# One-hot groups split around the scores, their multiply on GpSimd, and low weight halves kept in DRAM for the second dense stage

## The chip, the cores and the metric

The kernel runs on one core of a Trainium2 chip. A core has five engines that each work through their own instruction queue in order: TensorE (PE; its weight loads are shown apart as PEld), VectorE (DVE), ScalarE (ACT), GpSimd (POOL) and SyncE (SP), which here only issues DMAs. They meet through semaphores alone. The metric is the device time of one execution in microseconds (us).

## The reference

A layer norm feeds two branches, and their outputs and the input are added.

- Attention: S = 2048 positions, D = 512, 32 query heads of width 16 that share one key and one value head; exact softmax over all 2048 keys, then the product with `wo`.
- A product-key mixture of 4096 small experts (PEER): per position and head two scores over 64 keys each, the best two of each, the best two of their four sums; a softmax over these two gives the gates `g`. Each position so has 64 (expert, gate) pairs, and `out = sum g * gelu(x . u[e]) * v[e]`.

```python
act = _gelu(jnp.einsum("nd,nhkd->nhk", xf, ue))      # ue = u[top_e]
out = jnp.einsum("nhk,nhk,nhkd->nd", g, act, ve)     # ve = v[top_e]
return x + _A_ref(xn, ...) + _B_ref(xn, ...)
```

## The kernel before, in words

**Two ways through the experts.** The 2048 positions are four groups of 512. For groups 0 and 1 the experts are gathered: for each of 512 slots an indirect DMA from POOL's queue (L976, `gather`) brings 128 rows of u and v, DVE takes the dot product (L988, `dot`), ACT the tanh, and DVE adds the weighted v to the sum (L1023, `add`). Twelve buffers hold gathered rows; a gather waits until an add has freed one. For groups 2 and 3 the experts are computed densely (`dense`, run once with `DG` = 2 and once with `DG` = 3): all 4096 experts in `NB` = 32 blocks of 128, each block being 12 matmuls for the activations (L733), the gelu times a gate matrix, and the matmuls with v (L861).

**Halves.** Float32 products are made of faster fp32r matmuls: a tensor is split into a high half (a rounded copy) and a low half (what is left), and three of the four products are summed. For the expert weights `half_split` (L694) does this: ACT copies the high half out of the raw tile `rw` (L697), DVE subtracts to get the low one (L698). There are 64 such splits in each dense stage (u and v of 32 blocks). `fetch` (L664, L665) loads the raw tiles, two blocks ahead; with two buffers it has to wait until both engines are through with the tile that it overwrites.

**The gate matrix** of a dense stage is made at its start, in the one-hot stage. 512 positions are taken in `NQ` = 32 groups of `TB` = 16. For each group `onehot(q)` builds on DVE two one-hot tensors in fp16: `oa`, 128 x 2048 (L783), and `ob`, 128 x 512 (L785), and multiplies `ob` by the gate (L786). Then 16 small matmuls of 32 columns each (L815, `pg`) form the gate columns, and ACT copies the result out (L820). `onehot(q + 2)` is written two groups ahead of its matmuls; `obs` has three places for `ob`. When the gates are complete they go to DRAM, and the blocks follow.

**Order.** From the start of the attention loop on, the order on every engine is written out by hand. The loop has 256 steps of two key chunks. `att_steps` writes for each step: four scores matmuls (L326) and their two exponentials on ACT (L329), the 16 probability-times-value matmuls (L340, `pv`), then `mid()` (dots, tanh, deferred work), four scores matmuls and two exponentials again, then `fill()`. `fill` takes pieces of the expert work off the generator `score_thread` until its planned cost has caught up with a planned line (`aim`) or 4.0 (`MOST`) has been spent in this step. A one-hot group costs 2.0, so that a step of the one-hot stage (`dense_on[0] == 2`) takes two groups, both behind the second four scores matmuls. In that stage the adds and the next gathers (`go`) stand behind `fill`. Scores have two PSUM buffers, so a scores matmul waits for the exponential two before it.

Of the kernel before, what the change touches and what calls it, by code (L numbers as in the profile page):

```python
# [11 lines left out]
F32 = mybir.dt.float32  # L12
# [6 lines left out]
OP = mybir.AluOpType  # L19
# [4 lines left out]
P = 128  # L24
# [12 lines left out]
NSP = 2  # L37
NB = 32
# [12 lines left out]
MOST = 4.0  # L51
# [4 lines left out]
def tile_kernel(ctx, tc, x, wq, wkv, wo, wqT, kT, uv, ub, vb, out):  # L56
    nc = tc.nc
    pool = lambda name, **kw: ctx.enter_context(tc.tile_pool(name=name, **kw))
    dram = pool("dram", bufs=1, space=DRAM)
# [9 lines left out]
    raw = lambda ap: ap.bitcast(F32)  # L69
# [10 lines left out]
    d_m = dram.tile([2, H, S], F32, name="dm")  # L80
    d_sum = dram.tile([15, 8, 512], F32, name="dsum")
    d_inv = dram.tile([15, 8, 512], F32, name="dinv")
    d_part = [dram.tile([P, D], F32, name=f"dpart{t}") for t in range(NT)]


# [285 lines left out]
    def pair_load(pp):  # L371
        rc = small.tile([P, 32], F32, name="rc", bufs=1)
        nc.sync.dma_start(rc, d_sum[pp].rearrange("h n -> (h n)").rearrange("(p n) -> p n", n=32))
        RC[pp] = rc
# [68 lines left out]
    def out_ready():  # L443
        return PWO and GT * QB[PWO[0][0]] + PWO[0][1] in LIVE
# [28 lines left out]
    def wk_tile():  # L473
        return big.tile([P, 2, 512], F32R, name="wk", tag="wk", bufs=NWK)
# [181 lines left out]
    def dense(DG, after):  # L656
# [38 lines left out]
        def half_split(b, i):  # L695
            rw, w = raws[b], wk_tile()
            nc.scalar.copy(w[:, 0, :], rw[:, i, :])  # L697
            behind(lambda: nc.vector.tensor_tensor(out=w[:, 1, :], in0=rw[:, i, :], in1=w[:, 0, :], op=OP.subtract))  # L698
            return w

        def split(b):
# [74 lines left out]
        bc = lambda n, tb, w: tr[:, n, None, tb:tb + TB].to_broadcast([P, w, TB])  # L776
        OH = {}

        def onehot(q):
            if q < NQ:  # L780
                tb = q * TB
                oa = kt(F16, (P, P, TB))
                nc.vector.tensor_tensor(out=oa, in0=io, in1=bc(0, tb, P), op=OP.is_equal)  # L783
                ob = obs[:, q % 3]
                nc.vector.tensor_tensor(out=ob, in0=io[:, :NB, :], in1=bc(1, tb, NB), op=OP.is_equal)  # L785
                nc.vector.tensor_mul(ob, ob, bc(2, tb, NB))  # L786
                OH[q] = oa, ob

        def first_gates():
# [17 lines left out]
        for q in range(NQ):  # L807
# [4 lines left out]
            oa, ob = OH.pop(q)  # L812
# [223 lines left out]
    def dots(to):  # L1036
        while d_next[0] < min(to, NSL):
            dot(d_next[0])
            d_next[0] += 1
# [16 lines left out]
    store = STORES.append  # L1056
    on_act, behind = ON_ACT.append, BEHIND.append

    def run(fns):
        todo = fns[:]  # L1060
        fns.clear()
        for fn in todo:
            fn()

    def posts():
        while POST:
            for fn in POST.pop(0):
                fn()
# [50 lines left out]
    dense_on, quiet = [0], [0]  # L1119
    sgen = score_thread()  # L1120
    spent = [0.0]

    def run_scores(until=None, key=None):
        while (until is not None and spent[0] < until) or (key is not None and key not in IDX):
            posts()
            try:
                cost = next(sgen)
            except StopIteration:
                spent[0] = 1e9
                posts()  # L1130
                return
            if cost is None:

                if key is None:
                    return
                continue
            spent[0] += cost

    STEPS = 512


    def att_steps(d, mid, fill):
        i = 2 * d
        run(STORES)
        if 144 <= i < STEPS and i % 128 == 16:
            PWO.extend((i // 128 - 1, j) for j in range(4))
        if i < STEPS:
            u, kc = divmod(i, 16)
            if i == 0:
                load_q(0, rows=False)  # L1150
                run_scores(until=spent[0] + 1.8)
            if kc == 4 and u + 1 < 32:
                load_q(u + 1)
            scores(u, kc, 0)
            scores(u, kc, 1)
        if 0 < i <= STEPS:
            pu, pk = divmod(i - 2, 16)
            pv(pu, pk)
            pv(pu, pk + 1)
            if pk == 14:  # L1160
                unit_tail(pu)
        mid()
        if i < STEPS:
            scores(u, kc + 1, 0)
            scores(u, kc + 1, 1)
        if out_ready() and (i % 128 >= HOLD and PWO[0][0] != 1 or i % 128 >= 32 and i % 4 == 0 and PWO[0][0] == 1):
            block_out()
            spent[0] += 3.6
        fill()

        pp, r = divmod(i, 32)
        if pp and pp < 16:
            if r == 4:
                pair_load(pp - 1)
            if r == 6:
                pair_invert(pp - 1)
            if r == 10:
                pair_spread(pp - 1)
# [12 lines left out]
        if i == STEPS - 6:  # L1191
            load_last()
# [55 lines left out]
    with tc.manual_schedule(engines={E_.PE, E_.Activation, E_.DVE, E_.Pool, E_.SP}):  # L1248
        done0 = spent[0]
        half = STEPS // 2  # L1250
        pos, since = 0.0, half
        for d in range(half + 24):


            if dense_on[0] != 0:
                since = d
            if dense_on[0] == 1:
                pos += 2.6 if d < half * 3 // 4 else max(0.0, NSL - pos) / max(half - 3 - d, 1)
            else:
                pos += (2.1 if len(IDX) < NC * TPH else 2.3 if 0 <= d - since < 12 else 1.75, 0, 1.4, 1.5, 0.5)[dense_on[0]]  # L1260

            todo = max(min(int(pos + 0.001), g_next[0]) - d_next[0], 0)

            def mid():
                post = POST[:]
                POST.clear()
                for act, _ in post:
                    act()
                tanhs(d_next[0])
                run(ON_ACT)  # L1270
                ON_ACT.extend(LATER_ACT)
                LATER_ACT.clear()
                run(LAST)
                LAST.extend(LATER)
                LATER.clear()
                rest = BEHIND[:]
                BEHIND.clear()

                dots(d_next[0] + todo - 1)
                if a_ready[0] > a_next[0]:  # L1280
                    weigh(a_next[0] // SB)
                dots(d_next[0] + 1 if todo > 0 else 0)
                for _, fn in post:
                    fn()
                sums = min(a_ready[0] - a_next[0], max(todo, 3) if d < half else 4)
                if dense_on[0] > 2:
                    sums = min(sums, 2)
                if quiet[0] > 0:
                    quiet[0] -= 1
                    sums = 0  # L1290
                if dense_on[0] == 2:
                    run(CHAIN)

                def go():
                    n = sums
                    while rest or CHAIN or n > 0:
                        if n > 0:
                            adds(1)
                            n -= 1
                        elif not rest:  # L1300
                            run(CHAIN)
                        if CHAIN:
                            CHAIN.pop(0)()
                        if rest:
                            rest.pop(0)()
                    gathers(4)

                    for _ in range(1 if d < half - 4 else NT):
                        if OUTS:
                            experts_out(OUTS.pop(0))  # L1310

                if dense_on[0] == 2:
                    POST_FILL.append(go)
                else:
                    go()

            aim = done0 + (FILL - done0) * (d + 1) / half if d < half else 1e6

            def fill():
                run_scores(until=min(aim, spent[0] + MOST))  # L1320
                run(POST_FILL)

            att_steps(d, mid, fill)
        flush()
        run(STORES)
        while a_next[0] < NSL:
            dots(NSL)
            run(CHAIN)
            tanhs(d_next[0])
            adds(SB)  # L1330
            run(STORES)
            gathers(NGB)
        assert not OUTS
        run(STORES)
# [37 lines left out]
```

## Time and profile before

| | |
|---|---|
| median of 3 runs | 1931.54 us (1929.22 to 1931.95) |
| the profiled execution | 1925.78 us, span of its instructions 1924.1 us |
| PE, DVE, ACT, POOL busy | 97%, 85%, 67%, 36% of the span |
| first dense stage: one-hot groups | about 608 to 707 us |
| first dense stage: blocks | about 707 to 1100 us |
| second dense stage: one-hot groups | about 1413 to 1523 us |
| second dense stage: blocks | about 1523 to 1860 us |

The span runs from the first instruction to the last. Busy time of an engine is the time that it spends in instructions, waiting for operands within one included; a busy PE is not a PE at its peak. PEclk is the share of the TensorE clock that was granted. A line of groups reads: line, engine, operation, output<-input, shapes, count | busy us, mean ns of one | idle time before them and what ended it. A window line reads: window, its length, and for each engine busy us and (number of instructions).

### The profile page before, as it was taken

To read this page: it belongs to the slowest core of one execution; us is meant where nothing else is said; L and a number is where in the kernel's file an instruction comes from. 1 tells how busy PE (TensorE), PEld (TensorE's weight loads), DVE (VectorE), ACT (ScalarE), POOL (GpSimd) and SP (SyncE) were. 2 spreads that over 40 slices of the span, in tenths; PEclk is the share of its full clock that TensorE was granted. 3 is DMA by queue.
4 is the path that set the end of the run, shared out by engine and by line. 5 is a ranking of instruction groups with operands and counts; after the bars stand their busy time and mean duration, and the time that the engine had idled before them with its cause. 6 is when DMAs were issued, how large, how long until landed. Compare 5 with 4: busy or idle time off the path is not lost.

```text
span 1924.1 us, 34929 instructions
## 1 busy us (share of the span) xinstructions
PE 1863.8 (97%) x10990; PEld 991.8 (52%) x10990; DVE 1634.0 (85%) x6381; ACT 1294.2 (67%) x1803; POOL 700.8 (36%) x920
## 2 busy tenths in 40 slices
PE   6979999999999999999999999999999999999998
PEld 3634444555555554555555554555555455555553
DVE  6627787989998977999999897899988779999994
ACT  3346666655557887787877555555578777888873
POOL 1203334434452223343444444355422134344430
PEclk9989999999999899999999999999988899999999
DMA  7857789787773778888999987876736778899882
GB/s 274 315 186 278 266 272 301 279 296 251 249 246 122 233 240 249 253 288 270 287 300 309 362 287 237 280 256 220 242 105 220 249 215 292 271 284 286 282 277 84
DMA packets 234395, 491.13 MB, mean 255 GB/s; under 512 B 93396, under 2 KB 93396, under 8 KB 234204
## 3 DMA queue, kind: packets, MB, share of 16 engines
q0 software_dynamic: 73728, 268.47, 42.0%
q1 hardware_dynamic: 159240, 219.56, 34.9%
q8 instruction: 88, 1.44, 0.3%
q10 hardware_dynamic: 1236, 0.82, 0.1%
q14 instruction: 103, 0.84, 0.1%
HBM read 427.41 MB, written 56.07 MB: 251 GB/s over the span
## 4 chain that ended last, share of the span: by engine, by line
PE 85%; DMA 3%; ACT 3%; DVE 1%; issue 1%; SPq 0%; DVEq 0%; ACTq 0%
PE pv L340 24%; PE psc L531 18%; PE sc L326 17%; PE pact L733 9%; PE pout L861 9%; PE pg L815 3%; PE pwo L433 2%; ACT pt L329 2%; PE pw L486 1%; DMA wqt<-in_wqT_dram 1%; DMA dinv<-rc 1%; DMA wk<-dw 1%; PE pwt L493 0%; PE pwl L408 0%; DMA qa<-dqh 0%
## 5 line engine op out<-in xcount | busy, mean ns | idle before, releaser
L329 ACT ACTIVATE pt<-sc 128x1024 f32<-128x1024 f32 x1024 | 993.7, 1026 | 461.9 <-PE sc L326 460.5
L976 POOL DMA_INDIRECT g<-in_uv_dram,idx x512 | 556.8, 1087 | 1002.0 <-DVE xa L1023 531.0
L340 PE MATMUL pv<-pt,vaug 128*32 128x512 f32 x4096 | 516.4, 623 | 0.0
L531 PE MATMUL psc<-wk,xt 128*128 128x512 f32 x1536 | 388.7, 401 | 4.1 <-DVE wk L496 3.5
L326 PE MATMUL sc<-qa,kaug 64*128 64x512 f32 x2048 | 384.2, 451 | 8.6 <-ACT pt L329 8.4
L1023 DVE SCALAR_TENSOR_TENSOR xa<-g,w,xa 128x512 f32<-128x512 f32 x512 | 371.7, 744 | 0.1
L988 DVE CUSTOM_DVE_ANT_0 g<-g,xa 128x512 f32<-128x512 f32 x512 | 335.5, 681 | 7.4 <-DMA g<-in_uv_dram,idx 7.4
L531 PEld LDWEIGHTS psc<-wk,xt 128*128 128x128 f32 x1536 | 277.9, 188 | 107.7 <-issue 37.5
L326 PEld LDWEIGHTS sc<-qa,kaug 64*128 64x128 f32 x2048 | 155.9, 185 | 329.3 <-ACT pt L329 218.8
L340 PEld LDWEIGHTS pv<-pt,vaug 128*32 128x32 f32 x4096 | 109.6, 111 | 257.0 <-issue 255.4
L546 DVE FIND_INDEX8 i<-m,psc 128x8 uint32<-128x64 f32 x1024 | 206.3, 220 | 0.0
L733 PE MATMUL pact<-xt,wk 128*128 128x512 f32 x768 | 195.9, 400 | 0.0
L861 PE MATMUL pout<-wk,wd 128*128 128x512 f32 x768 | 194.8, 401 | 0.2 <-DVE wd L919 0.2
L544 DVE MAX8 m<-psc 128x8 f32<-128x64 f32 x1024 | 146.2, 213 | 41.1 <-PE psc L531 40.3
L861 PEld LDWEIGHTS pout<-wk,wd 128*128 128x128 f32 x768 | 140.8, 188 | 47.3 <-DVE act L988 5.5
L733 PEld LDWEIGHTS pact<-xt,wk 128*128 128x128 f32 x768 | 139.4, 188 | 48.5 <-issue 17.5
L698 DVE TENSOR_TENSOR wk<-rw,wk 128x512 fp32r<-128x512 f32 x128 | 84.8, 683 | 9.7 <-ACT wk L697 9.7
L864 DVE TENSOR_TENSOR da<-da,pout 128x512 f32<-128x512 f32 x128 | 82.8, 679 | 10.1 <-PE pout L861 10.0
L783 DVE TENSOR_TENSOR oh<-oh 128x2048 f16<-128x2048 f16 x64 | 78.0, 1219 | 0.8 <-ACT oh L759 0.6
L815 PEld LDWEIGHTS <-oh 128*128 128x128 f16 x1024 | 68.4, 162 | 13.8 <-issue 6.4
L1011 DVE SCALAR_TENSOR_TENSOR w<-gth,ga 128x4 f32<-128x4 f32 x128 | 20.4, 159 | 64.5 <-ACT gth L1004 64.0
L815 PE MATMUL pg<-oh 128*128 128x32 f16 x1024 | 73.5, 247 | 0.6 <-DVE oh L786 0.5
(159 smaller groups left out, 1411.1 us busy)
## 6 DMA issues: line engine op xcount, KB each, us to landing
wk<-dw SPq DMA_DIRECT2D x96, 512.0 KB
wqt<-in_wqT_dram SPq DMA_DIRECT2D x32, 512.0 KB
dw<-wk SPq DMA_DIRECT2D x32, 512.0 KB
rw<-in_ub_dram SPq DMA_DIRECT2D x64, 256.0 KB
rw<-in_vb_dram SPq DMA_DIRECT2D x64, 256.0 KB
gy<-dg SPq DMA_DIRECT2D x64, 256.0 KB
qa<-dqh SPq DMA_DIRECT2D x128, 64.0 KB
g<-in_uv_dram,idx POOLq DMA_INDIRECT x512, 6.0
```

What stands on the lines that cost most here:

```text
L326: nc.tensor.matmul(p[:, b, :], kaug[o:o + 64, kc * P:(kc + 1) * P], QA[u][o:o + 64, i, :], start=True, stop=True)
L329: nc.scalar.activation(pt, p, AF.Exp, scale=SCALE)
L340: nc.tensor.matmul(PV[u][32 * j:32 * j + 32, :], vaug[:, kc, :], pt[:, b, :], start=kc == 0, stop=kc == 15)
L531: nc.tensor.matmul(p, XT[g][k][:, a, j * P:(j + 1) * P], WC[n_][k][:, bb, :], start=n == 0, stop=n == 11)
L544: nc.vector.max(m8[:, jb, s, :], p[:, s * E:(s + 1) * E])
L546: nc.vector.max_index(i8[:, jb, s, :], m8[:, jb, s, :], p[:, s * E:(s + 1) * E])
L733: nc.tensor.matmul(p, us[:, a, k * P:(k + 1) * P], XT[DG][k][:, c, :], start=n == 0, stop=n == 11)
L815: nc.tensor.matmul(p[:, i * NB:(i + 1) * NB], oa[:, :, i], ob[:, :, i], start=True, stop=True)
L861: nc.tensor.matmul(p, wd[0][:, a, j * P:(j + 1) * P], vs[:, c, :], start=n == 0, stop=n == 5)
L976: nc.gpsimd.indirect_dma_start(out=gt, out_offset=None, in_=uv, in_offset=bass.IndirectOffsetOnAxis(ap=IDX[ph, c, ti][:, s:s + 1], axis=0))
L988: nc.vector.tensor_tensor_reduce(u, u, XN[TPH * ph + ti], scale=1.0, scalar=0.0, op0=OP.mult, op1=OP.add, accum_out=a[:, i:i + 1])
L1023: nc.vector.scalar_tensor_tensor(acc, v, w[:, i:i + 1], acc, op0=OP.mult, op1=OP.add)
```

## The change

Three things are changed, and no arithmetic.

1. In `onehot` the multiplication of `ob` by the gate is issued on GpSimd instead of VectorE: 64 instructions of 128 x 512 fp16, in place. It waits for the comparison that writes `ob`, and the group's small matmuls wait for it. In POOL's queue the 64 stand among the gathers.
2. In the one-hot stage a step's first group moves ahead of the second four scores matmuls: a new callback `between()` takes one piece off the generator there, and `fill` takes what is left of 4.0. PE's order in a step becomes scores, pv, group, scores, group; ACT's order stays as it was.
3. With `DG` = 2 each low half is also stored to a new DRAM tensor `d_lo` (64 DMAs of 256 KB, queued through `store` for the start of the next step). With `DG` = 3 the low half is loaded from there (64 DMAs of 256 KB from SP's queue) and the 64 subtractions on VectorE go. The raw weights are still loaded, for ACT's copy of the high half.

```diff
+    d_lo = dram.tile([NB, P, 2, 512], F32, name="dlo")
...
             nc.scalar.copy(w[:, 0, :], rw[:, i, :])
-            behind(lambda: nc.vector.tensor_tensor(out=w[:, 1, :], in0=rw[:, i, :], in1=w[:, 0, :], op=OP.subtract))
+            if DG > NSP:
+                nc.sync.dma_start(raw(w[:, 1, :]), d_lo[b, :, i, :])
+                return w
+
+            def low():
+                nc.vector.tensor_tensor(out=w[:, 1, :], in0=rw[:, i, :], in1=w[:, 0, :], op=OP.subtract)
+                store(lambda: nc.sync.dma_start(d_lo[b, :, i, :], raw(w[:, 1, :])))
+
+            behind(low)
             return w
...
-                nc.vector.tensor_mul(ob, ob, bc(2, tb, NB))
+                nc.gpsimd.tensor_mul(ob, ob, bc(2, tb, NB))
...
-    def att_steps(d, mid, fill):
+    def att_steps(d, mid, between, fill):
...
         mid()
+        between()
         if i < STEPS:
             scores(u, kc + 1, 0)
...
+            before = [0.0]
+
+            def between():
+                if dense_on[0] == 2 and spent[0] < aim:
+                    before[0] = spent[0]
+                    run_scores(until=spent[0] + 0.1)
+                    before[0] = spent[0] - before[0]
+
             def fill():
-                run_scores(until=min(aim, spent[0] + MOST))
+                run_scores(until=min(aim, spent[0] + MOST - before[0]))
                 run(POST_FILL)
```

More of the change, by code (lines that the diff above doesn't have):

```diff
@@ L1317, in tile_kernel @@
             aim = done0 + (FILL - done0) * (d + 1) / half if d < half else 1e6
+            before = [0.0]
[4 more added lines that the diff above has]
+                    before[0] = spent[0] - before[0]
             def fill():
-                run_scores(until=min(aim, spent[0] + MOST))
+                run_scores(until=min(aim, spent[0] + MOST - before[0]))
                 run(POST_FILL)
-            att_steps(d, mid, fill)
+            att_steps(d, mid, between, fill)
         flush()
```

## The prediction

> **What bounds the kernel now.** I read the page first: the chain that ended last, then the share of each engine.
>
> ```profile
> span 1924.1 us, 34929 instructions
> PE 1863.8 (97%) x10990; PEld 991.8 (52%) x10990; DVE 1634.0 (85%) x6381; ACT 1294.2 (67%) x1803; POOL 700.8 (36%) x920
> PE 85%; DMA 3%; ACT 3%; DVE 1%; issue 1%; SPq 0%; DVEq 0%; ACTq 0%
> ```
>
> The chain is PE's nearly throughout. But 97% is a mean over stages, and the change lies in four of them, so I then asked for busy times by stretch: first the two stretches of expert blocks, then the two one-hot stages.
>
> ```profile
> 1550.00:1850.00 300.00, 299.92 (x1683) 162.65 (x1682) 278.80 (x653) 236.91 (x336) 125.91 (x111) 1.00 0.88 276
> 750.00:1100.00 350.00, 349.00 (x1974) 192.00 (x1973) 326.43 (x852) 267.99 (x375) 142.97 (x133) 1.00 0.91 293
> 607.70:707.30 99.60, 98.42 (x921) 52.69 (x922) 95.08 (x199) 87.69 (x146) 21.47 (x18) 0.91 0.64 205
> 1413.50:1523.00 109.50, 107.22 (x922) 54.34 (x921) 96.17 (x195) 86.56 (x143) 24.15 (x20) 0.84 0.60 196
> ```
>
> (Busy us of PE, PEld, DVE, ACT, POOL, then PEclk, DMA share, GB/s.) In the blocks PE is idle for 0.08 of 300 and 1.0 of 350 us: nothing that relieves another engine can be worth more there. The one-hot stages, A (99.6 us) and B (109.5 us) below, differ. Three engines are near their limit, DVE with 95.1 and 96.2 us most of all, and the clock is below 1.00. The chain of work shows a step there at full and at lowered clock, and windows cut where the clock changes show how it is lowered:
>
> ```profile
> 614.53 2.17 PE pg L815 x32
> 616.70 0.66 PE sc L326 x4
> 617.36 1.85 PE pv L340 x16
> ...
> 619.88 2.17 PE pg L815 x32
> ...
> 640.80 2.21 PE pg L815 x32
> 643.00 0.66 PE sc L326 x4
> 643.67 3.54 PE pv L340 x16
> 647.21 0.66 PE sc L326 x4
> 647.87 2.17 PE pg L815 x32
> ```
>
> ```profile
> 643.68:647.10 3.42, 3.42 (x16) 0.52 (x16) 3.39 (x7) 1.82 (x2) 1.76 (x2) 0.50 0.99 279
> 647.10:650.51 3.41, 3.41 (x44) 2.76 (x40) 3.31 (x10) 3.25 (x7) 1.15 (x1) 1.00 1.02 407
> 650.51:653.92 3.41, 3.41 (x18) 0.59 (x16) 3.30 (x8) 2.75 (x6) 0.00 (x0) 0.50 0.68 248
> ```
>
> At full clock a step takes 5.35 us (614.53 to 619.88), with the lowered one 7.07 us (640.80 to 647.87); all of the difference is in pv, which falls into a stretch of 3.41 us at half clock after one that held the narrow group matmuls.
>
> **Part 1, the multiply on GpSimd.** What DVE saves: the multiplies of each stage, and from one start to the next what one takes of DVE's time:
>
> ```profile
> 607.70:707.30 99.60, 13.18 (x31) 0.91 0.64 205
> 1413.50:1523.00 109.50, 13.18 (x31) 0.84 0.60 196
> ...
> 657.06 0.42 DVE L785 TENSOR_TENSOR oh<-oh 128x512 f16<-128x512 f16 x1
> 657.51 0.43 DVE L786 TENSOR_TENSOR oh<-oh 128x512 f16<-128x512 f16 x1
> 657.85 0.74 DVE L1023 SCALAR_TENSOR_TENSOR xa<-g,w,xa 128x512 f32<-128x512 f32 x1
> ...
> 1413.50:1523.00 109.50, 2.06 (x3) 0.84 0.60 196
> ```
>
> Instructions overlap a little, so one costs 657.85 - 657.51 = 0.34 us, and 31 cost 10.5 us. In B 3 subtractions (the last row) go too by part 3, 2.1 us.
>
> What it costs: no GpSimd multiply of this size is in the trace, so I go by its small two-input ones, and by what happens when VectorE is busy.
>
> ```profile
> L603 POOL TENSOR_TENSOR e<-e,e x16: 217/684/719, 66.2 to 1235.1; 128x16 f32<-128x16 f32 x16
> L635 POOL TENSOR_TENSOR da<-hi,ii x32: 248/253/257, 450.3 to 1404.6; 128x32 f32<-128x32 f32 x32
> ```
>
> ```profile
> 250.12 0.68 DVE L988 CUSTOM_DVE_ANT_0 g<-g,xa 128x512 f32<-128x512 f32 x1
> 250.73 0.70 DVE L988 CUSTOM_DVE_ANT_0 g<-g,xa 128x512 f32<-128x512 f32 x1
> ...
> 183.04 0.75 DVE L988 CUSTOM_DVE_ANT_0 g<-g,xa 128x512 f32<-128x512 f32 x1
> 183.81 0.68 DVE L988 CUSTOM_DVE_ANT_0 g<-g,xa 128x512 f32<-128x512 f32 x1
> ```
>
> ```profile
> 250.24 0.64 POOL L600 TENSOR_TENSOR e<-fi 128x16 f32<-128x16 f32 x1
> 250.84 0.66 POOL L601 TENSOR_TENSOR e<-fi 128x16 f32<-128x16 f32 x1
> ...
> 183.02 0.22 POOL L604 TENSOR_TENSOR e<-e,cond 128x16 f32<-128x16 f32 x1
> ```
>
> Sixteen more elements take 31 ns more (min 217 to 248), so 512 take about 217 + 31 x 31 = 1180 ns, by rows that are far smaller and fp32. Beside a dot, whose two inputs both come from SBUF, the small ones take 0.64 and 0.66 us and end just behind the dot's end (250.88 and 250.80): GpSimd waits for VectorE. The other way round, L604 started 0.02 us ahead of the dot at 183.04, and this dot takes 0.75 us and the next 0.68: VectorE waits while GpSimd has the data, 0.07 us for 16 elements. For 512 that is 0.07 + 31 x 0.031 = 1.03 us for each multiply. Nearly all that DVE does in these stages (comparisons, dots, adds) has two SBUF inputs. The price lies between 0 us (a longer one holds nobody) and the whole 1.18 us; I take 1.03, worked from the only row that shows VectorE held.
>
> The page "SBUF — State Buffer" of the Trainium skill (section "SBUF: two separate sides") says that the two engines share a port pair as an exclusive lock, held for the whole instruction, that a VectorE instruction with two SBUF inputs needs it against a GpSimd one that reads SBUF, and that the loser blocks fully. By that rule 31 x 1.18 in place of 31 x 1.03 would add 5 us to each stage, 1968 us in all. The trace agrees on the waiting (0.22 against 0.64 us), and its one held dot (0.07 against 0.22 us) says that less than the whole instruction is held.
>
> So DVE in A: 95.1 - 10.5 + 31.9 = 116.5 us; in B: 96.2 - 10.5 - 2.1 + 31.9 = 115.5 us. Both are longer than the stages, so DVE sets their length. It is idle 4.5 us in A now; for waits at the stage's start (the first group now waits 1.2 us for its multiply in place of 0.43) and at each handover I leave 2 us, between 0 and 4.5. A: 118.5 - 99.6 = +18.9 us; B: 117.5 - 109.5 = +8.0 us. PE at half clock would need 16 x 7.07 = 113 us and stays just behind DVE. POOL adds 31 x 1.18 = 37 us of work to 21 and 24 and has room. A gather waits for an add that is written after the multiplies ahead of it, and the comparisons behind it are written after that add, so a multiply queued behind gathers loses a gather's own 1 us at most, and it is written a step ahead of its matmuls.
>
> **Part 2, the split.** PE and ACT get the same instructions; only PE's order changes, and the group's comparisons, multiplies and gate stores keep their places among the work of DVE, POOL and SP. At full clock a 3.41 us stretch can hold both halves and the scores between them (1.08 + 0.66 + 1.08 us), so as many narrow matmuls as before, and the lowered clock stays. It spreads PE's demands on ACT; with DVE as the bound this hides. I take 0, between +3 us a stage (the second scores now queue behind a group that waits for its multiply, 1.18 against 0.43 us for a few of the 16) and the first rival's gain.
>
> **Part 3, the low halves.** VectorE loses 54 of its subtractions in this stretch of the second stage's blocks, and gets 64 stores and 64 loads of 256 KB on SP's queue in exchange:
>
> ```profile
> 1550.00:1850.00 300.00, 35.81 (x54) 1.00 0.88 276
> ...
> q1 hardware_dynamic: 159240, 219.56, 34.9%
> ...
> 1050.00:1100.00 50.00, 49.61 (x280) 27.18 (x279) 45.24 (x194) 29.46 (x36) 21.54 (x26) 1.00 1.03 384
> ```
>
> The 35.8 us of DVE are worth 0, since PE is idle for only 0.08 us of those 300. The transfers: 64 x 256 KB = 16.8 MB; at the hardware queue's 34.9% x 1924.1 / 219.56 = 3.06 us per MB that is 51 us of all 16 engines, spread over some 450 us of each dense stage, a share of +0.11 on 0.88 to 0.91. The last row shows 1.03 with PE at 49.61 of 50, so I take 0 here too. On SP's queue a store stands behind the raw tiles' `fetch`, which waits for the same subtraction (L698) already, so it holds up nothing new; a load waits for a free `wk` tile, as ACT's copy of the other half does at the same place. The cover of both is that splits are made one to two blocks ahead; without it each late load would stop PE for a transfer of 0.8 us (3.06 x 0.26 MB), 51 us in all, which is the upper bound; the lower is 0.
>
> **The sum.** +18.9 + 8.0 + 0 + 0 = +27 us on the profiled execution: 1925.8 + 27 = 1952.7 us. That execution lies 5.8 us below the median of the runs, 1931.54 us, so I give 1931.5 + 27 = 1958 us. By the price's ends: with 1.18 us and no overlap +36, so 1968 us, and +6 from the split, 1974; with 0 the first rival.
>
> **The rivals.**
>
> *The multiply holds nobody (faster).* Then DVE needs 95.1 - 10.5 = 84.6 and 83.6 us, ACT its 87.7 and 86.6, and PE decides by its clock. Its pv in the two stages:
>
> ```profile
> 607.70:707.30 99.60, 39.58 (x272) 7.99 (x272) 0.91 0.64 205
> 1413.50:1523.00 109.50, 47.02 (x272) 8.75 (x272) 0.84 0.60 196
> ```
>
> At full clock 17 steps' pv take 17 x 1.85 = 31.5 us, so the lowered clock costs 8.1 and 15.5 us. With VectorE ahead and the groups split, all of it could go, with 1 and 2 us of idle PE: -27 us, 1905; with a quarter of it gone -6 us, 1926. I take the middle, -20 us: 1912 us. For it speaks that POOL has room; against it the dot of 0.75 us. It decides below a hold of about 0.6 us, where A's loss (84.6 + 31 x 0.6 + 2 = 105.2, +5.6 us) and B's gain (104.2, -5.3 us) cancel.
>
> *Half the hold (no change).* If fp16 elements pass two at a time, the hold is 0.07 + 0.48 = 0.55 us, DVE needs 101.7 and 100.7 us and 2 us of waits; A gains +4, B -7 by DVE but hardly that much with PE at 107.2 us. 1928 to 1935 us. No fp16 GpSimd row with two inputs is there to decide it.
>
> *The new transfers come late (slower).* A load that waits for its `wk` tile holds SP's queue, and behind it the next unit's queries (`qa`), without which PE stops. One such stop of half a step in every fourth step of the 46 that 1523 to 1850 us hold would cost about 40 us; that each tile is free when ACT copies now (DVE waited 9.7 us in all for that copy) speaks for far less, 10 us on top of the sum: 1968 us.
>
> ```profile
> L698 DVE TENSOR_TENSOR wk<-rw,wk 128x512 fp32r<-128x512 f32 x128 | 84.8, 683 | 9.7 <-ACT wk L697 9.7
> ```
>
> **How the numbers follow.** The hold of about 1 us: 0.64, at 1958 us, by itself 1940 to 1978. Late transfers on top: 0.06. Half the hold: 0.10, of which 0.03 slower, 0.05 within and 0.02 faster. No hold: 0.20. Slower by over 0.2% (about 4 us, what a measurement of this kernel can tell from no change): 0.64 + 0.06 + 0.03 = 0.73; within it 0.05; faster 0.02 + 0.20 = 0.22. The range 1910 to 1980 us leaves out the better half of the first rival (0.10) and 0.04 above.
>
> **What would show it.** Right: in both one-hot stages DVE's comparisons, dots and adds beside a GpSimd multiply last up to 1 us longer, or gaps of that size stand ahead of them; the multiplies last 1.2 us alone and up to 2.4 us behind a comparison; the stages measure about 118 us each and PE's groups wait for the multiply. The blocks of both dense stages keep their length, with DVE in the second at about 245 of 300 us. Wrong: multiplies of 0.7 us or less, or DVE's durations unchanged beside them; stages under 100 us with PEclk near 1.00; or PE idle in the blocks behind an SP load.

## The result and the profile after

The changed kernel takes 1997.65 us (median; 1987.02 to 2002.51) against 1931.74 us before on the same chip: a ratio of 1.0333, 95% interval 1.0306 to 1.0361. That is 66 us slower; the forecast was +27 us (1958) in a range of 1910 to 1980 us. The profiled execution is the fastest one, 1987.02 us, 61.2 us above the profiled one of before. From the page of the changed kernel (busy time of the engines; shares of the chain that ended last, by engine and by line):

```profile
PE 1892.7 (95%) x10990; PEld 1005.1 (51%) x10990; DVE 1619.3 (82%) x6253; ACT 1293.5 (65%) x1803; POOL 796.7 (40%) x984
...
PE 77%; DMA 6%; ACT 4%; issue 3%; DVE 2%; SPq 1%; POOL 0%; ACTq 0%; POOLq 0%; DVEq 0%
PE pv L341 22%; PE psc L532 18%; PE sc L327 15%; PE pout L870 8%; PE pact L742 7%; ACT pt L330 3%; DMA gy<-dg 3%; PE pg L824 2%; PE pwo L434 2%; PE pw L487 1%; DVE xa L1032 1%; DMA wqt<-in_wqT_dram 1%; DMA rw<-in_vb_dram 0%; PE pwt L494 0%; DVE g L997 0%
```

PE's share of the chain fell from 85% to 77%; DMAs have 6% of it instead of 3%, half of that the gate rows (`gy<-dg`), ACT's exponentials (`pt`) 3%. To place the loss I use the 256 attention steps: the first `pv` matmul of a step is found in every trace, so the same step can be compared. Stage A is steps 65 to 81 (17 steps), B is 183 to 199, the blocks of the first dense stage are steps 82 to 139, those of the second 200 to 254. Windows cut at these starts, first of before (A, B, and steps 115 to 132 of the first blocks), then of after (the same three, the second blocks, and 300 us of these; columns: window, length, busy us of PE, PEld, DVE, ACT, POOL, then PEclk, DMA share, GB/s):

```profile
611.00:709.35 98.35, 97.17 (x897) 51.29 (x895) 91.91 (x193) 86.39 (x145) 21.47 (x18) 0.92 0.65 208
1415.32:1524.20 108.88, 106.33 (x906) 53.36 (x904) 95.67 (x195) 86.66 (x144) 24.15 (x20) 0.84 0.60 199
939.35:1066.52 127.17, 126.56 (x716) 69.79 (x714) 119.50 (x281) 97.36 (x139) 52.79 (x47) 1.00 0.94 308
```

```profile
620.92:741.51 120.59, 113.73 (x897) 56.03 (x895) 100.97 (x163) 86.56 (x145) 71.25 (x50) 0.82 0.56 185
1470.01:1585.00 114.99, 107.24 (x907) 55.09 (x905) 105.63 (x160) 86.22 (x144) 76.75 (x51) 0.88 0.60 192
971.90:1120.77 148.87, 132.70 (x716) 72.91 (x714) 119.15 (x282) 97.59 (x139) 52.58 (x47) 0.95 0.92 309
1585.00:1953.00 368.00, 366.08 (x2048) 195.77 (x2046) 296.65 (x711) 286.44 (x405) 128.73 (x122) 1.00 0.93 307
...
1600.00:1900.00 300.00, 298.89 (x1674) 161.08 (x1670) 246.52 (x590) 235.28 (x333) 115.37 (x110) 1.00 0.96 319
```

A grew by 22.2 us, B by 6.1. In A VectorE, which should have become the bound with 116 us, is busy for only 101.0 of 120.6; the clock fell from 0.92 to 0.82, PE's busy time rose by 16.6 us for the same matmuls, and its idle time from 1.2 to 6.9 us. Steps 115 to 132 of the first blocks took 148.87 us in place of 127.17 (+21.7), and PE is idle there for 16.2 us. The second blocks, where VectorE lost its subtractions, are as long as before: PE is idle for 1.9 of 368 us. The remaining +11.0 us lie in steps outside these stages, 8.7 of them ahead of step 60, where no edited instruction has run yet; every other kernel below has +3 to +13 outside the stages too, so no edit is read into it (the profiled execution of before was 5.8 us below its median).

**GpSimd's multiply does hold VectorE.** The timeline of after around two of them (start, us, engine, line):

```profile
660.22 0.41 DVE L794 TENSOR_TENSOR oh<-oh 128x512 f16<-128x512 f16 x1
660.56 1.21 DVE L792 TENSOR_TENSOR oh<-oh 128x2048 f16<-128x2048 f16 x1
661.69 1.38 DVE L794 TENSOR_TENSOR oh<-oh 128x512 f16<-128x512 f16 x1
...
663.66 1.65 DVE L997 CUSTOM_DVE_ANT_0 g<-g,xa 128x512 f32<-128x512 f32 x1
```

```profile
660.72 2.07 POOL L795 TENSOR_TENSOR oh<-oh 128x512 f16<-128x512 f16 x1 [0.74 <-DVE oh L794]
663.15 1.60 POOL L795 TENSOR_TENSOR oh<-oh 128x512 f16<-128x512 f16 x1 [0.36 <-DVE oh L794]
...
L795 POOL TENSOR_TENSOR oh<-oh x64: 1156/1602/2081, 612.7 to 1580.0; 128x512 f16<-128x512 f16 x64
```

The multiply queued behind a comparison lasts 2.07 us, the shortest 1.156 us. A comparison that starts beside it takes 1.38 us instead of 0.41 (held 0.97 us), a dot 1.65 instead of 0.68.

**PE waits for exponentials.** PE's timeline of after; the bracket is idle time and who ended it:

```profile
659.03 1.21 PE L824 MATMUL pg<-oh 128*128 128x32 f16 x16
660.17 0.73 PE L327 MATMUL sc<-qa,kaug 64*128 64x512 f32 x4
660.84 1.24 PE L824 MATMUL pg<-oh 128*128 128x32 f16 x16
662.01 0.52 PE L327 MATMUL sc<-qa,kaug 64*128 64x512 f32 x2
662.77 0.50 PE L327 MATMUL sc<-qa,kaug 64*128 64x512 f32 x2 [0.24 <-ACT pt L330]
663.20 1.92 PE L341 MATMUL pv<-pt,vaug 128*32 128x512 f32 x16
```

The second scores of one step (660.17) and the first of the next (662.01) now have one group, 1.1 us, between them, where before both groups, 2.2 us, stood. Two exponentials take about 2 us (1.94 in the timeline of e8 below).

**The gate rows come late in the first blocks.** Chain of waits of after, two of five such pieces, and the wait list of steps 115 to 132, after and then before:

```profile
993.95 11.48 DMA gy<-dg
...
1020.86 12.25 DMA gy<-dg
```

```profile
DVE gy L913 <- DMA gy<-dg: 19.6, 5, 6.1
```

```profile
DVE gy L904 <- DMA gy<-dg: 3.2, 2, 2.1
```

(us in total, times, longest.) The gates of a block land 10 to 12 us after they were asked for; VectorE needs them for the block's product, and PE's next matmuls with v wait for that.

### The profile page after: what moved, and what is told of

Its sections match the earlier page's. It is cut to its first block, busy times and chain, and to the rows that moved or that the text cites. A ratio compares the mean times of both kernels' runs of the same rounds, so it can differ in the third digit from the quotient of the medians.

```text
span 1985.3 us, 35150 instructions
## 1 busy us (share of the span) xinstructions
PE 1892.7 (95%) x10990; PEld 1005.1 (51%) x10990; DVE 1619.3 (82%) x6253; ACT 1293.5 (65%) x1803; POOL 796.7 (40%) x984
## 4 chain that ended last, share of the span: by engine, by line
PE 77%; DMA 6%; ACT 4%; issue 3%; DVE 2%; SPq 1%; POOL 0%; ACTq 0%; POOLq 0%; DVEq 0%
PE pv L341 22%; PE psc L532 18%; PE sc L327 15%; PE pout L870 8%; PE pact L742 7%; ACT pt L330 3%; DMA gy<-dg 3%; PE pg L824 2%; PE pwo L434 2%; PE pw L487 1%; DVE xa L1032 1%; DMA wqt<-in_wqT_dram 1%; DMA rw<-in_vb_dram 0%; PE pwt L494 0%; DVE g L997 0%
## 5 line engine op out<-in xcount | busy, mean ns | idle before, releaser
L985 POOL DMA_INDIRECT g<-in_uv_dram,idx x512 | 546.2, 1067 | 886.3 <-DVE xa L1032 391.7
L327 PE MATMUL sc<-qa,kaug 64*128 64x512 f32 x2048 | 396.4, 458 | 19.9 <-ACT pt L330 18.6
L1032 DVE SCALAR_TENSOR_TENSOR xa<-g,w,xa 128x512 f32<-128x512 f32 x512 | 379.8, 761 | 0.1
L997 DVE CUSTOM_DVE_ANT_0 g<-g,xa 128x512 f32<-128x512 f32 x512 | 345.0, 699 | 13.1 <-DMA g<-in_uv_dram,idx 13.1
L870 PE MATMUL pout<-wk,wd 128*128 128x512 f32 x768 | 200.2, 409 | 15.8 <-DVE gy L913 8.9
L742 PEld LDWEIGHTS pact<-xt,wk 128*128 128x128 f32 x768 | 139.5, 188 | 50.2 <-issue 17.9
L795 POOL TENSOR_TENSOR oh<-oh 128x512 f16<-128x512 f16 x64 | 106.9, 1670 | 76.1 <-DVE oh L794 61.6
L873 DVE TENSOR_TENSOR da<-da,pout 128x512 f32<-128x512 f32 x128 | 82.8, 678 | 14.2 <-PE pout L870 14.1
L824 PE MATMUL pg<-oh 128*128 128x32 f16 x1024 | 79.1, 246 | 3.6 <-POOL oh L795 3.6
```

The source lines that it names most:

```text
L327: nc.tensor.matmul(p[:, b, :], kaug[o:o + 64, kc * P:(kc + 1) * P], QA[u][o:o + 64, i, :], start=True, stop=True)
L742: nc.tensor.matmul(p, us[:, a, k * P:(k + 1) * P], XT[DG][k][:, c, :], start=n == 0, stop=n == 11)
L824: nc.tensor.matmul(p[:, i * NB:(i + 1) * NB], oa[:, :, i], ob[:, :, i], start=True, stop=True)
L870: nc.tensor.matmul(p, wd[0][:, a, j * P:(j + 1) * P], vs[:, c, :], start=n == 0, stop=n == 5)
L985: nc.gpsimd.indirect_dma_start(out=gt, out_offset=None, in_=uv, in_offset=bass.IndirectOffsetOnAxis(ap=IDX[ph, c, ti][:, s:s + 1], axis=0))
L997: nc.vector.tensor_tensor_reduce(u, u, XN[TPH * ph + ti], scale=1.0, scalar=0.0, op0=OP.mult, op1=OP.add, accum_out=a[:, i:i + 1])
```

## The experiments

All are built from the kernel before. Times are medians; stages are differences to the profiled execution of before, by step starts as above.

| run | kernel | us (before on its chip) | ratio [95%] | A | blocks 1 | B | blocks 2 |
|---|---|---|---|---|---|---|---|
| change | all three parts | 1997.65 (1931.74) | 1.0333 [1.0306, 1.0361] | +22.2 | +21.5 | +6.1 | +0.4 |
| e1 | multiply on GpSimd | 1949.09 (1924.38) | 1.0139 [1.0105, 1.0174] | +11.5 | 0.0 | +2.6 | +0.3 |
| e2 | split | 1965.93 (1924.38) | 1.0234 [1.0199, 1.0269] | +23.1 | +0.7 | +14.7 | -0.8 |
| e3 | low halves | 1948.61 (1924.38) | 1.0140 [1.0113, 1.0167] | +0.8 | +24.3 | -7.0 | +1.1 |
| e4 | split and multiply | 1969.30 (1924.38) | 1.0222 [1.0175, 1.0269] | +26.3 | -0.7 | +7.7 | -1.0 |
| e5 | split, half pv | 1920.00 (1924.71) | 0.9973 [0.9957, 0.9989] | -2.5 | +0.7 | -9.7 | -0.3 |
| e6 | e5 and multiply | 1951.98 (1924.71) | 1.0144 [1.0127, 1.0161] | +13.8 | +0.2 | +7.1 | -0.2 |
| e7 | e1, multiplied twice | 2001.61 (1924.71) | 1.0405 [1.0387, 1.0422] | +39.7 | -0.1 | +31.2 | -0.5 |
| e8 | e3, stores from ACT's queue | 1973.99 (1924.71) | 1.0243 [1.0221, 1.0265] | +11.0 | +36.7 | -1.9 | +3.1 |
| e9 | e3, stores behind the gates | 1961.93 (1933.28) | 1.0167 [1.0134, 1.0199] | +21.1 | +11.2 | -9.6 | +0.8 |
| e10 | half pv, no split | 1938.24 (1933.28) | 1.0025 [1.0002, 1.0048] | +6.1 | +3.2 | -1.9 | -0.7 |
| e11 | e5 and e9 | 1944.46 (1933.28) | 1.0070 [1.0045, 1.0094] | +8.9 | +12.0 | -8.7 | +1.5 |
| e12 | e9 from the fifth block on | 1941.13 (1925.15) | 1.0077 [1.0052, 1.0102] | +0.1 | +15.9 | -13.4 | +4.4 |
| e13 | 3/4 pv, no split | 1940.88 (1930.48) | 1.0053 [1.0035, 1.0072] | +16.1 | +1.3 | -2.1 | -0.7 |
| e14 | 3/4 pv, split | 1944.79 (1930.48) | 1.0067 [1.0049, 1.0085] | +10.3 | +1.2 | +1.0 | -0.7 |

B differs by -13 to -2 us among e3, e8, e9 and e12, whose only edit there is three subtractions fewer; so less than some 10 us in B alone proves nothing.

### The three parts, one at a time: e1 to e4

e1, the multiply alone:

```diff
-                nc.vector.tensor_mul(ob, ob, bc(2, tb, NB))
+                nc.gpsimd.tensor_mul(ob, ob, bc(2, tb, NB))
```

> Only the multiply moves to GpSimd; one-hot groups stay unsplit, low halves stay on VectorE. Theory D (the prediction's: VectorE, held about 0.95 us by each GpSimd multiply, sets the length of both one-hot stages): +20 to +27 us over the kernel before, about 1955 us. Theory S (the one-hot stages of the changed kernel are long because the split makes PE and ScalarE wait for each other and lowers the clock; VectorE is idle for 18 of 120 us there): VectorE's need alone is about 106 to 110 us a stage, so +5 to +12 us, 1937 to 1944 us, nearly all in the first stage.

e2, the split alone: `between()` and its call as in the change's diff, the multiply on VectorE.

> Only the split: a step's first group moves ahead of its second scores; the multiply stays on VectorE. Theory D: VectorE has as much work as before, so 0 (within 6 us). Theory S: the second scores and the next step's first scores stand 1.1 us of group apart, less than the 2 us of two exponentials, so PE waits in each of 16 steps and the clock falls: +15 to +30 us over both one-hot stages, about 1955 us.

e3, the low halves alone: `d_lo`, the stores and the loads as in the change's diff.

> Only the low halves: 64 stores in the first dense stage, 64 loads in place of subtractions in the second. The prediction's step: 0 us. Theory G (the gate loads queue behind the new stores and come late; VectorE waits for them, then PE): +15 to +30 us, all between 950 and 1110 us in the blocks of the first dense stage, and 0 in the blocks of the second.

e4, the split and the multiply, without the low halves.

> Split and GpSimd multiply together, no low halves. If the parts add up and part 3 costs 21 us in the blocks, this is the changed kernel less about 25 us: 1965 to 1975 us. Theory D: as much as the multiply alone. Theory S: as much as the split alone, give or take 8 us.

Measured: +24.7, +41.5, +24.2 and +45 us. The multiply's total is near its forecast (+27), but that is in part luck: only 14.1 us lie in A and B, which were to grow by 26.9, and of the 9.4 us outside the four stages 6.9 are there by step 60, before any multiply has run. By the stages theory S's +5 to +12 was nearer, and nearly all in A as it said. The two parts that were put at nothing cost 41 and 24 us: the split in A and B, more than theory S's +15 to +30, and the low halves in the blocks of the first stage alone, as theory G had it. Split and multiply together cost hardly more than the split (45 against 41): both stretch the same steps, and VectorE, idle for 25.5 us of A when both are in, has time to catch up while PE waits or runs slowly. With the low halves' 24 us that makes 69, the change's +66. Windows of A: multiply alone, split alone, both:

```profile
619.45:729.26 109.81, 104.34 (x897) 53.39 (x895) 104.77 (x163) 86.77 (x145) 72.27 (x50) 0.85 0.60 197
```

```profile
614.42:735.83 121.41, 115.03 (x896) 56.28 (x894) 92.64 (x193) 86.16 (x146) 21.46 (x18) 0.79 0.51 170
```

```profile
622.82:747.50 124.68, 118.45 (x896) 56.80 (x894) 99.16 (x163) 86.18 (x145) 70.80 (x50) 0.76 0.54 177
```

With the split alone PE is idle for 6.4 us (before: 1.2), and its busy time is 17.9 us more for the same matmuls, at a clock of 0.79 against 0.92. The 5.2 and the 17.9 us are the whole 23.1 us. By the wait lists of A, the split's and then before's (us in total, times, longest), the idle time is that of scores matmuls behind an exponential:

```profile
PE sc L326 <- ACT pt L329: 6.4, 15, 0.9
```

```profile
PE sc L326 <- ACT pt L329: 1.2, 4, 0.4
```

With the multiply alone VectorE is busy for 104.8 of 109.8 us, and the clock is lower too (0.85). The groups of A show where most of the hold falls, on the comparisons that write `ob`; before, then e1:

```profile
L785 DVE TENSOR_TENSOR oh<-oh 128x512 f16<-128x512 f16 x29 | 12.1, 418 | 0.0
```

```profile
L785 DVE TENSOR_TENSOR oh<-oh 128x512 f16<-128x512 f16 x29 | 25.5, 881 | 0.0
```

### Is it the hold? e7

```diff
                 nc.gpsimd.tensor_mul(ob, ob, bc(2, tb, NB))
+                nc.gpsimd.tensor_mul(obs[:, 3], ob, bc(2, tb, NB))
...
-        obs = kt(F16, (P, 3, NB, TB))
+        obs = kt(F16, (P, 4, NB, TB))
```

> The multiply alone on GpSimd, and GpSimd does each multiply a second time into a part of the tile that nobody reads. Theory D (the loss is VectorE held 0.96 us for each multiply): another 32 holds in each stage, so A and B each 20 to 30 us longer than with one multiply; 1949 + 40 to 60 = 1989 to 2009. Rival L (the loss is that the groups wait for a multiply that comes later): the second multiply only lengthens POOL's queue, +0 to +12 us, 1949 to 1961.

Measured 2001.61 us, +52 on e1 (each against before on its chip), inside what the hold would give and far outside rival L's +0 to +12. A grew from 109.81 to 138.02 us, by 28.2 for 30 more multiplies, 0.94 us each, and VectorE is now the bound that the forecast made of it, busy for 137.25 of 138.02 us:

```profile
613.47:751.49 138.02, 119.67 (x896) 56.77 (x894) 137.25 (x164) 87.59 (x145) 116.11 (x80) 0.74 0.48 157
```

By the Trainium skill, "SBUF — State Buffer" (section "SBUF: two separate sides"), the loser waits for the whole instruction. The runs show 0.94 to 0.97 us of 1.156, so the measurement decides for somewhat less.

### What costs in the split? e5, e6, e10, e13, e14

e5 keeps the split, but puts one of a step's two `pv` halves behind the second scores; e6 is e5 with the multiply on GpSimd:

```diff
             pv(pu, pk)
-            pv(pu, pk + 1)
...
+            half_pv = dense_on[0] == 2 and i < STEPS
+            if not half_pv:
+                pv(pu, pk + 1)
...
         mid()
         between()
         if i < STEPS:
             scores(u, kc + 1, 0)
             scores(u, kc + 1, 1)
+        if 0 < i <= STEPS and half_pv:
+            pv(pu, pk + 1)
```

> The split alone, with the multiply on VectorE, but in the one-hot stages only one of a step's two pv halves stands ahead of the first group and the other behind the second scores, so that PE's order is scores, half pv, group, scores, half pv, group. Theory W (the split loses because its second scores and the next step's first ones stand only one group, 1.1 us, apart, less than the two exponentials of 1.03 us that free their PSUM buffers, and PE's waits pull the clock down): with about 0.93 + 1.1 = 2.0 us between any two pairs the waits go, and every 3.41 us stretch holds wide matmuls, so the clock stays up: A and B between no change and 8 and 15 us shorter than before, 1900 to 1925 us. Rival N (a split group costs by itself, wherever the pv stands): as the split alone, +25 to +45 us, 1950 to 1970.

> As the half-pv order, and the multiply on GpSimd. Theory W with the hold: PE no longer waits on exponentials, VectorE's 116 us become the bound that the prediction had: A +12 to +22 us and B 0 to +10 against before, 1935 to 1955 in all, VectorE idle under 5 us in A. Rival (the hold matters only together with PE's waits): as the half-pv order without GpSimd, within 8 us of it.

e5 is 4.7 us faster than before, by a ratio whose interval (0.9957 to 0.9989) does not reach 1; it is the only kernel here that is faster than before. The split's loss is gone. Windows of A and B:

```profile
615.91:711.77 95.86, 93.74 (x896) 50.03 (x895) 92.32 (x194) 86.58 (x145) 21.46 (x18) 1.00 0.65 214
1418.23:1517.45 99.22, 94.94 (x906) 50.20 (x904) 95.22 (x195) 87.05 (x144) 23.82 (x20) 0.98 0.67 217
```

The clock is 1.00 and 0.98 (before 0.92 and 0.84). With that out of the way the multiply costs 1951.98 - 1920.00 = 32 us, near the 27 that the prediction had for it, and here A and B do hold it (16.3 and 16.7 us more than in e5); in A VectorE is busy for 104.56 of 112.16 us, so idle for 7.6, a little more than the 5 that I had expected.

e10 keeps the half `pv` and takes the split away:

```diff
-                if dense_on[0] == 2 and spent[0] < aim:
+                if False:
```

> The half-pv order without the split: scores, half pv, scores, half pv, both groups; the multiply on VectorE. Now it is the first and the second scores of a step that stand only half a pv (0.93 us) apart, and no group is split. Theory W (what costs is two pairs of scores closer than two exponentials): PE waits about 1 us in each of the 17 steps of a stage and the clock falls as with the split: A +12 to +30, B +5 to +25, 1940 to 1975 in all. Rival N (a split group costs by itself): no split, so within 8 us of before.

Theory W failed as I had put it. PE does wait, for 7.1 us of A, a little more than in the split, though 0.4 us a step and not the 1 us that W had; but the clock is 0.98 (0.94 in B), A is only 6.1 us longer than before, and B 1.9 us shorter:

```profile
617.12:721.61 104.49, 97.39 (x896) 50.23 (x895) 91.71 (x193) 86.83 (x145) 21.48 (x18) 0.98 0.61 196
```

Rival N's number, within 8 us of before, came out, but e5 has the split and loses nothing, so N's reason is out as well. Waits of 7 us need not lower the clock. Theory C took W's place (a stretch of 3.41 us without `pv` lowers it), and e13 and e14 were to test it: three quarters of `pv` ahead of the second scores, one quarter behind them.

```diff
+            pv(pu, pk + 1, (0,) if half_pv else (0, 1))
...
+            pv(pu, pk + 1, (1,))
```

> As the unsplit half-pv order, but three quarters of a step's pv stand between the first and the second scores and one quarter behind the second: scores, 3/4 pv (1.39 us), scores, 1/4 pv, both groups; multiply on VectorE. Theory C (the clock is halved after a 3.41 us stretch without pv; waits for exponentials only add their own length): longest stretch without pv 2.17 + 0.66 = 2.8 us, clock 0.95 or more in A and B; pairs 1.39 us apart in place of 0.93, so PE idle in A between 2 and 7.1 us: A 96 to 103, B 100 to 112, 1918 to 1934 in all. Rival W (waits pull the clock down): clock between the 0.98 of the half-pv orders and the 0.92 of before, with no tie to where pv stands.

> The split with three quarters of pv ahead of the first group and one quarter behind the second scores: scores, 3/4 pv, group, scores, 1/4 pv, group. The second scores and the next first ones stand 0.46 + 1.1 = 1.56 us apart, between the split alone (1.1 us, clock 0.79) and the split with half pv (2.0 us, clock 1.00), so PE waits for exponentials in nearly every step. Theory C: longest stretch without pv 1.8 us, so the clock is 0.97 to 1.00 in both stages in spite of the waits: A 95 to 101, B 97 to 108, 1915 to 1930. Rival W: a clock of 0.85 to 0.95, A 100 to 112, 1930 to 1950.

Both missed their times, for a reason of their own. PE's timeline of e14:

```profile
642.43 1.91 PE L340 MATMUL pv<-pt,vaug 128*32 128x512 f32 x12
644.28 1.24 PE L815 MATMUL pg<-oh 128*128 128x32 f16 x16
645.45 0.73 PE L326 MATMUL sc<-qa,kaug 64*128 64x512 f32 x4
646.11 1.05 PE L340 MATMUL pv<-pt,vaug 128*32 128x512 f32 x4
```

Four `pv` matmuls take 1.05 us, as long as the eight of a half (1.06), and twelve as long as sixteen (1.91). A `pv` matmul writes one of four strips of 32 partitions (`pv` in the code), and a quarter has only two of the four; the single records of the traces show that the strips work side by side: before, four `pv` matmuls start within 0.02 us of each other and the next four 0.45 us later; in e14's quarter two start 0.006 us apart and the next two 0.45 us later. The price is 1 us for each of 17 steps, and it put the pairs of scores more than two exponentials apart, so e14 has hardly any waits (1.3 us of A) and can't tell theirs from the clock. The clocks of A, e13 and then e14:

```profile
616.78:731.24 114.46, 114.46 (x897) 54.04 (x895) 92.06 (x193) 87.92 (x145) 21.44 (x18) 0.91 0.55 179
```

```profile
616.41:725.02 108.61, 107.36 (x896) 53.58 (x895) 91.94 (x193) 86.72 (x145) 21.48 (x18) 1.00 0.60 189
```

e13 settles one thing: its clock in A is 0.91 while PE is never idle (by the profile, in which the ends of matmuls are modelled). The Trainium skill, "TensorE: Matmul & The Clock Gate" (section "What's actually happening"), gives half clock after at least one idle window of about 3.4 us; here the clock is halved in such windows without idle time. But C expected 0.95 or more for this order in both stages and is wrong too (0.98 in B). What stands, with the multiply on VectorE: with one group alone between pieces of `pv` (e5, e14) the clock was 0.98 to 1.00, with whole `pv` 0.78 to 0.92 (before and e2), the split the lowest, and e10 and e13 lie between (0.91 to 0.98). In e6, where PE's groups also wait for GpSimd's multiply (11.4 of 12.4 us idle in A), e5's order had 0.92:

```profile
614.48:726.64 112.16, 99.72 (x896) 51.49 (x895) 104.56 (x163) 86.76 (x145) 72.26 (x50) 0.92 0.59 192
```

Which property of a stretch halves the clock of the next one stays open, so it is shown that the order of the split costs 17.9 us of A through the clock, and not why.

### What costs in the low halves? e8, e9, e11, e12

e8 issues the stores from ACT's queue:

```diff
-                store(lambda: nc.sync.dma_start(d_lo[b, :, i, :], raw(w[:, 1, :])))
+                store(lambda: nc.scalar.dma_start(d_lo[b, :, i, :], raw(w[:, 1, :])))
```

> The low halves alone (multiply and split as before), with the stores issued on ACT's DMA queue in place of SP's. Theory G-order (the gate rows come late because they stand behind the stores on SP's queue): blocks of the first dense stage between 0 and +6 us, 1924 to 1932 in all (ACT pays 64 issues, unless that holds its copies). Rival G-traffic (the transfers together are too much in these blocks, whatever queue): the blocks again +20 to +25, 1944 to 1952.

The wait for the gates did go, from 22.5 us in steps 115 to 132 of e3 to 2.3, but the blocks lost 36.7 us, A 11.0, and the total lies above both ranges. A store in ACT's queue holds what is behind it, exponentials among it, until VectorE, with its earlier work, has made the low half. ACT's timeline and wait list in e8:

```profile
1021.42 0.96 ACTq L705 DMA_DIRECT2D dlo<-wk  x2
1022.76 1.94 ACT L330 ACTIVATE pt<-sc 128x1024 f32<-128x1024 f32 x2 [2.29 <-DVE da L873]
...
ACT pt L330 <- DVE da L873: 11.8, 4, 3.4
```

The time can't decide, so e9 leaves bytes and queue as they were and changes the order alone; the held stores are queued in `fetch_gates`, behind the gate rows' DMA:

```diff
-                store(lambda: nc.sync.dma_start(d_lo[b, :, i, :], raw(w[:, 1, :])))
+                lows.append(lambda: nc.sync.dma_start(d_lo[b, :, i, :], raw(w[:, 1, :])))
...
                 fetched.add(b)
+            STORES.extend(lows)
+            lows.clear()
```

> The low halves alone, all of it on SP's queue as in the change, but in the first dense stage each block's two stores are issued in the step after the next block's gate rows have been asked for, not before. Same bytes, same queue, other order. Theory G-order (the gate rows come late because the stores stand ahead of them): the first stage's blocks between 0 and +8 us, VectorE's wait for the gate rows under 6 us there against 23.2 with the stores ahead; 1924 to 1933 in all. Rival G-traffic (too much in flight in these blocks, whatever the order): the blocks again +15 to +25, 1940 to 1950.

> The split with half a pv on each side and the late stores together, the multiply on VectorE: the change with its three losses taken out. Theories W, D and G-order: no part of the +66 is left, 1912 to 1926. If G-traffic holds: +15 to +25 of the blocks stays, 1935 to 1945.

Steps 115 to 132, e3 and then e9:

```profile
944.20:1095.58 151.38, 135.09 (x716) 73.72 (x715) 119.15 (x281) 97.40 (x139) 53.52 (x47) 0.93 0.90 303
```

```profile
969.45:1096.63 127.18, 126.57 (x716) 69.79 (x714) 119.36 (x282) 97.52 (x139) 54.54 (x47) 1.00 1.01 349
...
DVE gy L915 <- DMA gy<-dg: 5.3, 3, 2.2
```

In e9 these 18 steps take 127.18 us, in before 127.17, while more bytes pass than in e3 (349 against 303 GB/s). So it was the order: the gates stood behind half a megabyte of stores. The Trainium skill, "DMA: Bandwidth & Descriptors" (section "Queues, rings and completion order"), has each DMA engine consume a queue's descriptors in order; the trace agrees, with 22.5 us of waits for the gates behind the stores and 5.3 ahead of them. The totals of e9 and e11 missed all the same, +28.7 and +11 us (e11's lies where G-traffic had it), and so did the blocks, +11.2 and +12.0, since the late stores held something else: A grew by 21.1 us in e9 with no edit to its work, in its last steps, where one-hots and block weights share the `wk` buffers with tiles that still waited for their store. e12 holds a store back only after five blocks' gates have been asked for:

```diff
-                lows.append(lambda: nc.sync.dma_start(d_lo[b, :, i, :], raw(w[:, 1, :])))
+                (lows.append if len(fetched) > 4 else store)(lambda: nc.sync.dma_start(d_lo[b, :, i, :], raw(w[:, 1, :])))
```

> As the late stores, but a store is held back only once the gate rows of five blocks have been asked for; until then it is issued at once, as in the change. Before, stores held back since the one-hot stage kept the wk tiles that its own one-hots and the first blocks wait for (A +19.8, steps 106 and 107 +4.5 us). If that is what those were: A within 8 us of the 99.6 us it has with the stores at once, steps 81 to 110 within 2 us of before, steps 110 to 131 within 2 us by G-order, and +5 us left near step 134, where the projection weights wait on SP's queue behind a row that waits for a store of sums to land; 1927 to 1940 in all. If the low halves' traffic itself is what costs: 1945 or more.

A is back at +0.1 us, so the held stores were the reason there. But the blocks keep 15.9 us in four single steps: 84 (+3.9), 106 (+2.9), 115 (+4.1, the first late gates) and 134 (+5.0, projection weights behind a row that waits for a stored sum). Both forecasts "within 2 us" missed: steps 110 to 131 by step 115, and steps 81 to 110, 6.7 us longer, by steps 84 and 106, so that what holds step 106 is not a store held since the one-hot stage. The time, 1941 us, is just over the 1927 to 1940 expected, and 16 us above before. So the order is shown to be the cause of what e9 and e12 took out of steps 115 to 132, 24.2 and 20.0 of 24.2 us; the rest, in other single steps, has causes that I read from the waits and did not test.

## Why the prediction was wrong, step by step

- **The blocks are PE's, so part 3's 35.8 us of VectorE are worth nothing: right.** The second blocks moved by 0.4 us, although VectorE is busy there for 246.5 of 300 us, as forecast (245).
- **The multiply's hold: the mechanism right, the price somewhat too high.** Forecast 1.03 us of VectorE a multiply, and 1.18 for a multiply alone; measured 1.156 at the least for the multiply, 0.97 for the comparison shown and 0.94 for each that e7 added. In e1 it is about 0.77, an estimate: VectorE's busy time of A went from 91.91 to 104.77 us although 30 multiplies of 0.34 us had left it. So A got 11.5 for 18.9 and B 2.6 for 8.0, and the total of +24.7 us is nearer to +27 than the stages are. The rivals that had it hold nobody, or half, are out. So is the mechanism "DVE sets the stages' length" for the change itself: with the split it is idle for 19.6 us of A.
- **That price was partly luck.** It was scaled up from one fp32 dot held for 0.07 us, called "the only row that shows VectorE held". Other dots beside small GpSimd instructions say otherwise: before, the one at 218.18 us starts 0.14 us behind an instruction of 0.23 us and takes 0.68 us, so it is not held at all, and others take up to 0.74 us.
- **The split at 0: the step that failed, by 41 us.** The text reasoned that it "spreads PE's demands on ACT; with DVE as the bound this hides". It does the reverse: moving a group ahead of the second scores leaves one behind them, 1.1 us, which is less than the two exponentials that the next scores wait for. And the forecast that the lowered clock "stays" was wrong: 0.92 went to 0.79 in e2. The upper bound, +3 us a stage, thought only of a group that waits for its multiply; with the multiply on VectorE the stages lost 23.1 and 14.7 us, and A took 121.4 us, PE's 115.0 busy and 6.4 waiting, more than the 118.5 us that VectorE was to need. I had checked how many narrow matmuls a 3.41 us stretch can hold, and not what else is in it; what in it sets the clock is still open.
- **The transfers at 0: the other step that failed, by 24 us, all of it in the first blocks.** The sentence "it holds up nothing new" looked at the raw tiles' fetch, which waits for the same subtraction, and not at the gate rows queued behind the stores, which had no slack. The 51 us upper bound for late transfers was put on the loads; these cost nothing. The rival of late transfers had the right kind of cause at the wrong place, with 0.06.
- **The sum.** The three parts alone add to 90 us and give 66 together, since split and multiply share their steps (45 together). The forecast's +27 was the one part that had a row to be worked from.

## What to carry to other kernels

Work moved between two uses of a double buffer must be laid against the consumer's time on both sides: here 1.1 us stood where two exponentials needed 2. An added store is cheap by its bytes and dear by its place: look for the load behind it in the same queue that has the least slack, and for the buffer that it keeps. And when parts of a change overlap in the same steps, only runs of each part alone tell which of them costs.

## What the runs showed of the hardware that I had not expected

- TensorE's clock is halved in single stretches of 3.41 us while PE has matmuls all the time (e13's A: 0.91 with 0.00 us idle), and taking `pv` in halves around the groups brought it from 0.92 and 0.84 to 1.00 and 0.98 with the same matmuls.
- Four `pv` matmuls on two strips take as long (1.05 us) as eight on four strips (1.06).
- With 256 KB stores ahead of them in the same queue the gate rows landed 10 to 12 us after their issue (the change), and the steps that need them took 24 us longer at a mean DMA share no higher than before (e3, 0.90 against 0.94); with the stores behind them those steps took no longer (e9).
